# Strassen's products on 512-row blocks, and whole sequences convolved and routed at once, in a convolution with a gated mixture of experts

## The chip, the cores and the metric

The kernel runs on one core of a Trainium2 chip. The core has a matrix engine (PE, with its weight loads shown apart as PEld), a vector engine (DVE), a scalar engine (ACT), a general engine (POOL), a queue engine (SP), 16 DMA engines, an on-chip memory SBUF of 128 partitions, and PSUM, eight banks of 512 fp32 columns in which matmuls accumulate. The metric is the device time of one execution in microseconds; the kernel before takes 1325.93 us (median of three runs, 1324.46 to 1328.33).

## The reference

Eight sequences of 3,584 tokens with 192 channels are filtered and then go through one expert each:

```
out1[b,s,:]  = sum over k of softmax(weight)[head,k] * x[b, s-6+k, head]      # causal, 7 taps, 8 heads of 24 channels
logits       = out1 @ w_gate                  (8 experts)
fresh        = argmax(logits);  free = sigmoid(out1 @ w_local) < 0.5 or s == 0
expert[b,s]  = fresh if free else expert[b,s-1]                               # a chain along the sequence
out[b,s,:]   = softmax(logits)[expert] * (relu(out1 @ w1[expert]) @ w2[expert])   # 192 -> 1024 -> 192
```

All of it is fp32. There are 28,672 tokens.

## The kernel before

The tokens are cut into 16 groups of 1,792 (`NPART`, `PT`), two to a sequence. Groups 0 and 1 take a special path through PE (`wide`, `wide_route`), so that expert work can begin early. The other 14 take these stages:

- **Convolution** (`conv`, L366): each partition holds 14 successive tokens (`NT`) and their halo. For each of the 8 heads ACT writes the first tap (L377), and DVE adds six more, one instruction each (L387).
- **Logits** (`logits`, L565): DVE transposes the rows into `z` (L570), PE multiplies by the gate weights in 48 small matmuls (L580) into two tiles of the pool `hps_p`, ACT copies them out (L585), DVE turns them back (L588, L596).
- **Routing** (`route`, L601, and `table`): some 90 small DVE instructions find each token's expert and its slot in a table in DRAM, `slots`, in which each expert has its own stretch.
- **Puts** (`put`, L768): POOL scatters rows to `slots`, 128 at a time, by indirect DMA.

Expert work goes by blocks of rows of one expert. A unit is 128 rows; a block is one unit ("single") or two ("pair"). The list `blocks` is fixed when the program is built: 35 singles, then 87 pairs, then 20 singles, 229 units in all. Which expert a block belongs to is read from a table at run time. Two spare singles run at the end only if an entry asks for them. For each block SP loads the expert's weights (`load_w`, 1.5 MB, three blocks ahead, four buffers) and the rows (`load_rows`). PE transposes the rows (`turn`, L359), ACT copies them to `xT` (L949). `hidden` (L952) does the first layer: PE works with two tiles of 64 rows side by side, so 24 matmuls of 64 x 128 weights against 64 x 256 columns for a pair run as 12 concurrent couples; an fp32 matmul shows as two records. ACT applies relu (L968). `output` (L973) does the second layer: 16 matmuls of 192 columns per unit. ACT scales one half of the sum (L988), DVE scales and adds the other (L992), POOL scatters the result (L996).

The order is written out by hand in the main loop (L1138): every engine executes its instructions in the order in which the program issues them. Conv and route are generators; each `yield` gives a price in microseconds, and `step(t)` (L1037) issues about `t` us worth of them on DVE between the pieces of a block: 1.2 + 2.1 + 1.3 per single, 1.2 + 4.2 + 3.0 per pair. `ensure` (L1090) issues such work early and whole where a block needs a group that is not routed yet.

Of the kernel before, what the change touches and what calls it, by code (L numbers as in the profile page):

```python
# [33 lines left out]
NX = NT + HALO  # L34
# [4 lines left out]
KT = BT // P  # L39
# [4 lines left out]
EARLY = 3  # L44
SPARE = 2

# [5 lines left out]


ONE = [_sure(min(g + 1, EARLY) * PT, UT) for g in range(NPART)]
TWO = [_sure((g + 1) * PT - ONE[-1] * UT, BT) if g >= EARLY else 0 for g in range(NPART)]


HALF = 0.5
FULL = {0: ONE[0], HALF: _sure(PT + PT // 2, UT), **{g: ONE[g] for g in range(1, NPART)}}
REST = NU - ONE[-1] - 2 * TWO[-1]  # L60
# [21 lines left out]
def kernel(  # L82
# [13 lines left out]
    xs = ctx.enter_context(tc.tile_pool(name="xs", bufs=2))  # L96
    ys = ctx.enter_context(tc.tile_pool(name="ys", bufs=4))
# [3 lines left out]
    xp = ctx.enter_context(tc.tile_pool(name="xp", bufs=6))  # L101
    tp = ctx.enter_context(tc.tile_pool(name="tp", bufs=1))
    hp = ctx.enter_context(tc.tile_pool(name="hp", bufs=1))
    op = ctx.enter_context(tc.tile_pool(name="op", bufs=2))
    xps_p = ctx.enter_context(tc.tile_pool(name="xps_p", bufs=1, space=PSUM))
    hps_p = ctx.enter_context(tc.tile_pool(name="hps_p", bufs=4, space=PSUM))
    yps_p = ctx.enter_context(tc.tile_pool(name="yps_p", bufs=2, space=PSUM))
# [6 lines left out]
    def load_x(g):  # L114
        x_sb = xs.tile([P, NX, D], F32, name="x_sb")
        src = x[g // PER]
        win = bass.AP(tensor=src.tensor, offset=src.offset + g % PER * PT * D,
                      ap=[[NT * D, P], [1, NX * D]])
        nc.sync.dma_start(out=x_sb.rearrange("p t d -> p (t d)"), in_=win)
        return x_sb  # L120

    def load_b(g):

        x_sb = xs.tile([P, NX, D], F32, name="x_sb")
        xv = x_sb.rearrange("p t d -> p (t d)")[:, :NB * D].rearrange("p (b d) -> p b d", d=D)
        for b in (slice(0, NH), slice(NH, NB)):
            nc.sync.dma_start(out=xv[:, b, :], in_=xb[g, :, b, :])
        return xv
# [9 lines left out]
    with tc.tile_pool(name="scr", bufs=1) as scr:  # L138
# [4 lines left out]
        x_in = {0: load_b(0)}  # L143
        wg = cst.tile([P, 3 + DQ, Q], F32, name="wg")
        nc.sync.dma_start(out=wg, in_=wgl)
        x_in[1] = load_b(1)
# [43 lines left out]
    def z_tile():  # L190
        return yt.tile([P, 3 * NH * TB + NB * DR], F32, name="z")
# [3 lines left out]
    def wide(g, xv, y_sb, both):  # L195
# [58 lines left out]
        yr = zy[:TB, 3 * NH * TB:].rearrange("p (b d) -> p b d", d=DR)  # L254
# [17 lines left out]
        lt = sm.tile([P, NB, E + 1], F32, name="lt")[:TB]  # L272
# [9 lines left out]
    pi = cst.tile([P, 2], I32, name="pi")  # L282
# [83 lines left out]
    def conv(g, x_sb):  # L366
# [14 lines left out]
        for h in range(H):  # L381
            if h + 1 < H:
                first(h + 1)
# [850 lines left out]
```

## Time and profile before

| | |
|---|---|
| median of three runs | 1325.93 us |
| the profiled execution, its span | 1326.81 us, 1325.1 us |
| busy: PE, DVE, ACT, POOL | 1304.4, 778.3, 625.2, 480.4 us |
| granted PE clock | 0.998 |
| first expert matmul begins; last output matmul ends | 46.16; 1318.3 us |
| HBM read, written | 277.3 MB, 45.8 MB |

A group's line gives its source line, engine, operation, tiles, shapes and count, then busy time (the union of its instructions' intervals) and the mean duration of one. Matmuls overlap, so their mean is longer than busy time divided by count. The list by slices has one digit for each fortieth of the span, the busy share in tenths. The table by stages gives busy time and count per engine in a stretch. The timeline gives start, duration, engine, line and count of merged instructions.

### The profile page before, as it was taken

Reading aid. Unit: us, or ns where it says so; the run is one execution under the profiler, and the core shown is the slowest. Engines: PE = TensorE matmul, PEld = TensorE weight load, DVE = VectorE, ACT = ScalarE, POOL = GpSimd, SP = SyncE. Lnnn points to the kernel's source line nnn. Section 1 sums busy time; section 2 is a strip of 40 time slices with the busy share of each in tenths; the row PEclk is TensorE's granted clock in tenths of the full one; section 3 lists DMA queues with packets and bytes.
Section 4 is the critical chain, followed back from the end, with each engine's and each line's share of the span. In section 5 each row is a group of like instructions: output and inputs, shape, how many; then the busy total and the mean of one; then the engine's idle time right before and its main releaser. Section 6 shows DMA issues by size and latency. Waiting matters only on the chain. (4 is left out here: it accounts for less than half of the span.)

```text
span 1325.1 us, 41356 instructions
## 1 busy us (share of the span) xinstructions
PE 1304.4 (98%) x16682; PEld 1260.9 (95%) x16682; DVE 778.3 (59%) x2434; ACT 625.2 (47%) x1571; POOL 480.4 (36%) x520
## 2 busy tenths in 40 slices
PE   9899999999999999999999999999999999999997
PEld 7799999999999999999999999999999999999997
DVE  6888898977878787878777878785610000000000
ACT  5345555544454545444545454544444444444553
POOL 4445352534343434343434343434344212211111
PEclk9999999999999999999999999999999999999999
DMA  5789999967575757575757575756565555556893
GB/s 188 283 349 391 376 365 345 394 213 266 182 275 177 290 188 277 201 260 192 271 186 273 193 271 199 267 195 210 197 211 205 189 185 188 192 187 229 313 317 131
DMA packets 67298, 325.29 MB, mean 245 GB/s; under 512 B 12576, under 2 KB 38103, under 8 KB 47650
## 3 DMA queue, kind: packets, MB, share of 16 engines
q1 hardware_dynamic: 44784, 277.41, 58.4%
q0 software_dynamic: 22320, 45.22, 9.2%
q8 instruction: 133, 2.18, 0.7%
q14 instruction: 59, 0.48, 0.1%
q10 hardware_dynamic: 2, 0.00, 0.0%
HBM read 277.29 MB, written 45.77 MB: 244 GB/s over the span
## 5 line engine op out<-in xcount | busy, mean ns | idle before, releaser
L980 PE MATMUL yps<-wb,hT 64*128 64x192 f32 x7328 | 641.0, 325 | 5.8 <-ACT hT L968 2.8
L963 PE MATMUL hps<-xT,wb 64*128 64x256 f32 (+1 forms) x6816 | 637.2, 336 | 1.7 <-issue 1.4
L963 PEld LDWEIGHTS hps<-xT,wb 64*128 64x128 f32 x6816 | 589.1, 187 | 27.2 <-issue 4.0
L980 PEld LDWEIGHTS yps<-wb,hT 64*128 64x128 f32 x7328 | 602.8, 187 | 11.1 <-issue 4.6
L996 POOL DMA_INDIRECT out_dram<-o_sb,xg x229 | 232.3, 1014 | 605.7 <-DVE o_sb L992 533.9
L968 ACT ACTIVATE hT<-hps 128x512 f32<-128x512 f32 (+1 forms) x568 | 261.9, 512 | 361.4 <-PE hps L963 246.5
L387 DVE SCALAR_TENSOR_TENSOR y_sb<-x_sb,c,y_sb 128x336 f32<-128x336 f32 x672 | 376.5, 570 | 18.9 <-issue 0.8
L992 DVE SCALAR_TENSOR_TENSOR o_sb<-yps,xg,o_sb 128x192 f32<-128x192 f32 x229 | 87.5, 414 | 467.8 <-ACT o_sb L988 461.4
L775 POOL DMA_INDIRECT slots<-y_sb,posi x228 | 231.2, 1014 | 209.3 <-ACT xT L949 114.8
L988 ACT ACTIVATE o_sb<-yps,xg 128x192 f32<-128x192 f32 x229 | 86.9, 418 | 289.8 <-PE yps L980 287.4
L949 ACT COPY xT<-xps 64x256 f32<-64x256 f32 (+4 forms) x568 | 210.8, 371 | 11.7 <-issue 1.7
L377 ACT ACTIVATE y_sb<-x_sb,c 128x336 f32<-128x336 f32 x112 | 63.7, 581 | 0.0
L359 PEld LDWEIGHTS xps<-ident,xg 64*128 64x128 f32 (+1 forms) x916 | 57.0, 124 | 5.2
L359 PE MATMUL xps<-ident,xg 64*128 64x64 f32 (+1 forms) x916 | 60.0, 217 | 0.0
L570 DVE STREAM_TRANSPOSE z<-y_sb 128x768 f32<-128x768 f32 (+1 forms) x56 | 45.4, 853 | 0.4
L596 DVE COPY lt<-lq 32x36 f32<-32x36 f32 x224 | 40.8, 182 | 3.5
L580 PE MATMUL hps<-z,wg 64*32 64x128 f32 x1344 | 24.2, 272 | 1.2 <-issue 1.2
L580 PEld LDWEIGHTS hps<-z,wg 64*32 64x32 f32 x1344 | 19.2, 105 | 4.1 <-issue 2.9
L556 PE MATMUL yps<-y_sb,hot 112*128 112x194 f32 x64 | 12.6, 353 | 1.4 <-DVE hot L550 1.1
L556 PEld LDWEIGHTS yps<-y_sb,hot 112*128 112x128 f32 x64 | 11.3, 202 | 2.1 <-DVE hot L550 1.6
L672 DVE COPY bk<-so_far 1x32 f32<-1x32 f32 x56 | 12.3, 220 | 0.7
L588 DVE STREAM_TRANSPOSE lq<-ls 128x256 f32<-128x256 f32 x14 | 6.2, 441 | 10.9 <-ACT ls L585 10.9
(236 smaller groups left out, 358.0 us busy)
## 6 DMA issues: line engine op xcount, KB each, us to landing
wb<-in_w_dram SPq DMA_DIRECT2D x138, 1536.0 KB
x_sb<-in_x_dram SPq DMA_DIRECT2D x14, 1920.0 KB
xg<-slots SPq DMA_DIRECT2D x87, 195.0 KB
wb<-in_w_dram SPq DMA_DIRECT2D x12, 512.0 KB
xg<-slots SPq DMA_DIRECT2D x53, 97.5 KB
out_dram<-o_sb,xg POOLq DMA_INDIRECT x229
slots<-y_sb,posi POOLq DMA_INDIRECT x228
x_sb<-in_xb_dram SPq DMA_DIRECT2D x4, 768.0 KB
```

Of the source, the lines that this page charges most:

```text
L359: nc.tensor.transpose(to, src[rows], identity=ident[rows, rows])
L377: nc.scalar.activation(cols(h), chans(h, 0), Act.Copy, scale=c[:, h, 0:1])
L387: nc.vector.scalar_tensor_tensor(cols(h), chans(h, k), c[:, h, k:k + 1], cols(h), Alu.mult, Alu.add)
L570: nc.vector.transpose(z[:, t:u, :], y_sb[:, t:u, Y0:Y0 + D])
L775: ins = nc.gpsimd.indirect_dma_start(out=slots[:, :], in_=rows, in_offset=None, out_offset=bass.IndirectOffsetOnAxis(ap=to, axis=0)).ins
L949: copied = nc.scalar.copy(a, b)
L963: nc.tensor.matmul(hps[half][:, j, w], lhsT=wb[rows, f0:f0 + P], rhs=xT[rows, d, w], start=(d == 0 and j == 0), stop=(d == KD - 1), skip_g ...
L968: relu = nc.scalar.activation(hT[:, m:m + 2, w], hps[half][:, :, w], Act.Relu)
L980: nc.tensor.matmul(yps[half][:, k * D:(k + 1) * D], lhsT=hT[rows, m, k * P:(k + 1) * P], rhs=wb[rows, WA + m * D:WA + (m + 1) * D], start= ...
L988: nc.scalar.activation(o_sb[:, k, :], y[k][0], Act.Copy, scale=xg[:, k, 0:1])
L992: nc.vector.scalar_tensor_tensor(o_sb[:, k, :], y[k][1], xg[:, k, 0:1], o_sb[:, k, :], Alu.mult, Alu.add)
L996: sent = nc.gpsimd.indirect_dma_start(out=out, in_=o_sb[:, k, :], in_offset=None, out_offset=bass.IndirectOffsetOnAxis(ap=xg.bitcast(I32)[ ...
```

## The change

It has four parts, and the seven products are new code.

- **Blocks.** `EARLY` goes from 3 to 4: singles come first from four groups. The list is now 51 singles, 20 pairs, 31 blocks of four units ("fours"), 14 singles: again 229 units. The fixed list now assumes more than the worst case guarantees (`_likely` with `LEFT`...), and 28 spare singles stand under two conditions at the end.
- **Seven products.** For a four, `seven` replaces `hidden`: the first two chunks of 64 channels, the two halves of the hidden units and the two halves of the rows form a 2 x 2 by 2 x 2 product, done with 7 products in place of 8; the third chunk takes 4. `combine_x` makes the sums of inputs on DVE, `combine_w` those of weights on POOL, and DVE adds three of the results.
- **Sequences.** From group 4 on, a whole sequence (28 tokens per partition) is convolved and routed at once; inputs are loaded by quarters of the channels (`load_x`, issued by ACT within `taps`), and the first taps are issued in `taps`.
- **PSUM.** In place of `hps_p` (4 banks), `yps_p` and `xps_p` (2 each) there are four pools of one tile of two banks: `wps_p` (transposes), `xps_p` and `yps_p` (hidden), `zps_p` (output). The logits take the pool that `step` is given.

```diff
+NS = 2 * NT
-EARLY = 3
+EARLY = 4
+XG = 5
+FIRST = 8
+PAIRED = 20
+LEFT1 = 640
+LEFT2 = 1408
+LEFT = 2900
+LEFT3 = 1152
...
-    def load_x(g):
+    def load_x(u, queue=None):
...
+        (queue or nc.scalar).dma_start(out=x_sb.rearrange("p t d -> p (t d)"), in_=win)
...
+    def taps(most):
+        u = len(x_in)
+        if u < len(UNITS):
+            depth = 3 if UNITS[u][0] < EARLY else 2
+            if u - depth <= st["unit"] - (st["cgen"] is not None):
+                load_x(u)
+        for u in (st["unit"], st["unit"] + 1):
...
+                    tap(u, j)
...
+                nc.vector.scalar_tensor_tensor(cols, x_in[u][:, k:k + n, j * GS:(j + 1) * GS],
+                                               c[:, h, k:k + 1], cols, Alu.mult, Alu.add)
+                yield 0.6 if n == NT else 1.0
...
+            yield "pe"
+            both = st["bank"].tile([P, 2, 512], F32, name="ps")
+            lps = [both[:, half, :TQ * Q] for half in range(2)]
+            for b in range(DQ):
+                if b == DQ // 2:
+                    yield "half"
...
+    def combine_w(wb):
+        wt = hp.tile([P, 3, 2 * P], F32, name="wt")
+        b11, b12, b21, b22 = [wb[:, k * 2 * P:(k + 1) * 2 * P] for k in range(4)]
+        nc.gpsimd.tensor_tensor(wt[:, 1, :], b22, b12, op=Alu.subtract)
+        nc.gpsimd.tensor_tensor(b12, b12, b11, op=Alu.subtract)
+        nc.gpsimd.tensor_tensor(wt[:, 0, :], b22, b12, op=Alu.subtract)
+        nc.gpsimd.tensor_tensor(wt[:, 2, :], b21, wt[:, 0, :], op=Alu.subtract)
+        return wt
+
+    def combine_x(xT):
+        xc = hp.tile([P, 4, HU * P], F32, name="xc")
+        one, two = slice(0, HU * P), slice(HU * P, KT * P)
+        nc.vector.tensor_tensor(xc[:, 0, :], xT[:, 0, one], xT[:, 0, two], op=Alu.subtract)
+        nc.vector.tensor_tensor(xT[:, 0, two], xT[:, 0, two], xT[:, 1, two], op=Alu.add)
...
+    def seven(wb, wt, xT, xc, turn_next, weights_next):
...
+        def times(to, a, b, first=False):
+            for j in range(2):
+                for half, rows in halves():
+                    nc.tensor.matmul(to[:, half, j, :], lhsT=b[rows, j * P:(j + 1) * P],
+                                     rhs=a[rows, :], start=(first and j == 0), stop=True,
+                                     skip_group_check=True)
+        times(xb, a11, b11, True)
+        puts_by(nc.scalar.copy(h11, xb))
+        times(yb, s1, t1, True)
+        times(yb, a23, b32)
+        puts_by(nc.scalar.copy(h22, yb))
+        times(xb, s2, t2)
+        nc.scalar.copy(h12, xb)
+        times(wbk, a12, b21, True)
+        times(wbk, a13, b31)
+        step(SIDE[0])
+        nc.vector.tensor_tensor(h11, wbk, h11, op=Alu.add)
+        nc.scalar.activation(h11, h11, Act.Relu)
+        times(xb, s3, t3)
+        nc.vector.tensor_tensor(h22, xb, h22, op=Alu.add)
+        nc.scalar.activation(h22, h22, Act.Relu)
+        times(yb, s4, b22)
+        times(yb, s5, b32)
+        at = turn_next()
+        times(xb, a22, t4)
+        wt = weights_next()
+        times(xb, a23, b31)
+        nc.vector.tensor_tensor(h12, yb, h12, op=Alu.add)
+        puts_by(nc.scalar.activation(h12, h12, Act.Relu))
+        nc.scalar.activation(h21, xb, Act.Relu)
...
+    def output(n, wb, xg, hT, rows_next=None):
+        for part, h in enumerate(hT):
+            m = min(n, HU)
+            y_p = zps_p if part == len(hT) - 1 else yps_p
...
+            if rows_next and part == 0:
+                taps(min(n, 2))
+            step((1.3 if n > 1 or st["block"] else 0) if n < KT else SIDE[2 + part],
+                 wps_p if n < KT or part == 0 else None)
...
+            if part == 0 and rows_next:
+                rows_next()
+    SIDE = (2.0, 4.4, 1.6, 1.4)
...
+        if n == KT:
+            hT, at, wt = seven(wbs[i], wt, xT, xc, turn_next, weights_next)
+        else:
+            hT = hidden(n, wbs[i], xT, (1, 1) if i else (0, 0))
+            wt = weights_next()
+            at = turn_next()
...
+        step(2.4 if i == 0 else {1: 2.3, 2: 4.7, 4: SIDE[1]}[n], zps_p if n == KT else xps_p)
+        output(n, wbs.pop(i), xgs.pop(i), hT, rows_next)
...
+        if n < KT:
+            step(1.4 if n == 1 else 3.6)
```

## The prediction

> **What bounds the kernel now.** I read the busy shares and the forty slices first, then the groups by shape, then the stages, then PE's timeline.
>
> ```profile
> PE 1304.4 (98%) x16682; PEld 1260.9 (95%) x16682; DVE 778.3 (59%) x2434; ACT 625.2 (47%) x1571; POOL 480.4 (36%) x520
> ...
> PE   9899999999999999999999999999999999999997
> ...
> DVE  6888898977878787878777878785610000000000
> ```
>
> PE is busy in every slice; DVE is nearly full only up to a quarter of the span. Whether busy PE is also PE at its rate, the groups by shape and the timeline tell:
>
> ```profile
> L980 PE MATMUL yps<-wb,hT 64*128 64x192 f32 x7328 | 641.0, 325 | 5.8 <-ACT hT L968 2.8 <-DVE o_sb L992 1.9 <-issue 0.9
> L963 PE MATMUL hps<-xT,wb 64*128 64x256 f32 x4176 | 472.5, 376 | 0.0
> L387 DVE SCALAR_TENSOR_TENSOR y_sb<-x_sb,c,y_sb 128x336 f32<-128x336 f32 x672 | 376.5, 570 | 18.9 <-issue 0.8
> L968 ACT ACTIVATE hT<-hps 128x512 f32<-128x512 f32 x348 | 189.5, 595 | 288.9 <-PE hps L963 204.2 <-PE xps L359 78.9 <-issue 5.8
> L992 DVE SCALAR_TENSOR_TENSOR o_sb<-yps,xg,o_sb 128x192 f32<-128x192 f32 x229 | 87.5, 414 | 467.8 <-ACT o_sb L988 461.4 <-DMA xg<-slots 5.0 <-PE hps L963 0.9
> L968 ACT ACTIVATE hT<-hps 128x256 f32<-128x256 f32 x220 | 72.5, 381 | 72.5 <-PE hps L963 42.3 <-PE xps L359 14.4 <-ACT o_sb L988 7.8
> ```
>
> PE's own waits are 5.8 us of 641 in the second layer and nothing in the pairs' first layer; ACT and DVE wait for PE. Here is PE's timeline, first through two pairs, then two singles near the end:
>
> ```profile
> 271.04 5.34 PE L963 MATMUL hps<-xT,wb 64*128 64x256 f32 x47
> 276.04 0.39 PE L359 MATMUL xps<-ident,xg 64*128 64x64 f32 x5
> ...
> 281.70 5.34 PE L963 MATMUL hps<-xT,wb 64*128 64x256 f32 x47
> ```
> ```profile
> 1302.00 2.84 PE L963 MATMUL hps<-xT,wb 64*128 64x128 f32 x48
> ...
> 1307.44 2.84 PE L963 MATMUL hps<-xT,wb 64*128 64x128 f32 x48
> ```
>
> A pair takes 281.70 - 271.04 = 10.66 us, a single 5.44 us, always. A pair's first layer spans about 5.18 us for 12 couples (0.43 us per couple of 256 columns). The stages, with their busy times for PE, PEld, DVE, ACT and POOL, then clock, DMA share and GB/s, show where something else presses:
>
> ```profile
> 46.00:257.00 211.00, 203.97 (x3227) 198.43 (x3227) 185.67 (x562) 112.50 (x351) 95.22 (x94) 1.00 0.94 357
> 257.00:1209.00 952.00, 950.66 (x11505) 917.77 (x11503) 552.07 (x1742) 435.01 (x984) 343.70 (x339) 1.00 0.62 220
> 1209.00:1326.00 117.00, 109.07 (x1678) 108.48 (x1674) 9.10 (x22) 55.37 (x178) 21.44 (x22) 0.99 0.74 259
> ```
>
> The pairs' stage is PE alone: 87 x 10.66 = 927, 11 logits at about 1.9 (a pair with logits takes 12.5 us) = 21, leaving 4 of 952 us. The early singles are tighter: 35 x 5.44 = 190 and 3 logits at 2.3 = 7, so 14 of 211 us are lost there, with DVE 88% and DMA 94% busy. The last 20 singles lose nothing. So time is the count of matmuls, plus what the early singles lose.
>
> **What the Trainium skill says.** "FP8 and Floating Point Precision", section "TensorE Precision Notes", counts four passes for true fp32; the trace fits passes by columns, 0.43 us for 256 and about 0.33 for 192 (5.3 us for the pair's 16 couples), so a saved couple of 256 is worth its whole 0.43. "SBUF — State Buffer", section "SBUF: two separate sides", says that a POOL operation that reads SBUF and a DVE operation with two SBUF inputs lock each other out for the whole instruction. The trace before has too little POOL arithmetic to show this. "GPSIMD Engine Reference", section 3.1, prices an fp32 tensor_tensor at 4497 ns for 2,048 columns; the trace has only a POOL copy of 512 in 655 ns. "VectorE: DVE Perf Modes", on the SBUF errata, gives (N + 151)/0.96 ns for an fp32 tensor_tensor; the trace's scalar_tensor_tensor of 336 took 570 ns where that gives 507.
>
> **The change part by part.**
>
> *Units.* Both lists hold 229 units. Whether the tables fill is a matter of the seeded data: routed as the reference does, the experts get 3,274 to 4,253 tokens, every planned single, pair and four is full when its group is routed, and 1,152 tokens remain, exactly 14 singles. The 28 spares should not run.
>
> *Seven products, the gain.* A four's first layer is 11 products of two couples, 22 in place of 24: 2 x 0.43 = 0.85 us saved. Its second layer (64 matmuls) and 16 transposes are those of two pairs. So a four is 2 x 10.66 - 0.85 = 20.47 us. The new list against the old: 10 more singles, 67 fewer pairs, 31 fours: 10 x 5.44 - 67 x 10.66 + 31 x 20.47 = 54.4 - 714.2 + 634.6 = **-25.2 us**.
>
> *What a four asks of the others.* ACT: a 1,024-column read from PSUM, estimated from the two relu rows, (595 - 381)/256 = 0.84 ns per column, is about 1.02 us, or 0.97 with the uncontended 0.54 for 512 in the timeline. Three copies and four relus make 7, the four xT copies 2.7, o_sb 1.7, taps up to 1.9: 13 of 20.5 us. DVE: slope (570 - 414)/144 = 1.08 ns per column, so an add from PSUM of 1,024 is 1.3 us; three are 3.9; combine_x by the page's formula 5 x 0.42 = 2.1; four o_sb 1.7; the steps 2.0 + 4.4 + 1.6 + 1.4 = 9.4. Sum 17.1, and if POOL locks it out during combine_w, 4 x 0.56 (page, in proportion) to 4 x 0.8 more: 19.3 to 20.3. That just fits. POOL: up to 8 puts and 4 scatters at 1.01 plus 2.6 = 15.
>
> *Does any of it stand in PE's way?* Starting a four at 0 with products of 0.86: xb ends at 0.86, its ACT copy at 2.1, and PE writes xb again at 2.6: 0.5 spare. The copy of yb ends at 3.8, that of xb at 4.7; PE wants xb at 5.2: 0.4 spare. wbk ends at 5.2, the DVE adds of h11 and h22 at 6.7 and 8.0; transposes need wps at 7.8 and product a22 t4 needs xb at 8.4: 0.4 spare. h12 leaves yb at 9.3, wanted at 10.2. combine_x ends about 18.5 (20.5 with the lock), wanted at 21.3; combine_w has 10 us. So nothing stalls in the mean, with half a microsecond of slack at three places. In the fours that still carry conv and route (about 14, from the count below) I charge 0.25 us each, 3.5; bounds 0 and 1.5 each.
>
> *Conv and routing.* A 672-column tap is 570 + 336 x 1.04 = 920 ns for two of 570. The yields of a sequence sum to about 72 (48 conv, 24 route and tables) where two groups took 98. Counting steps against that, puts and blocks in order of issue, all groups are ready in time (one `ensure` at the first pair finds only a put missing), and conv and route are through by four number 14. DVE thus falls empty at about 830 us. Off PE's path this is worth nothing. Logits mostly get the bank wps after an output, whose next user is a whole first layer away: free. Two parts fall on xps, which the next block's first layer wants while ACT still does o_sb, a tap and the two copies: about 1 us each, 2.
>
> *Early singles.* Now 51 with DVE work, each carrying 2.3 + 1.3 + 1.4 = 5.0 in steps for 4.6. With o_sb that is 5.4 of 5.44 us, and only the logits' pauses let DVE breathe; DMA must bring 1.54 MB of weights, 0.1 rows and some 0.23 (was 0.18) of x per single. The first blocks already lose most of the 14 us, so 16 more singles at 0.2 each add 3; bounds 0 and 20 (0.4 each for 51). The moved x loads are issued by ACT behind o_sb; one that waited for DVE's last tap would hold ACT's relus and so PE, but that tap was issued before the output it follows. About 0 each; in the 20 bound.
>
> *Start and end.* Order and counts of the `wide` path stay; PSUM pools are only renamed, 0 +- 2. The last 14 singles are as before.
>
> *Sum.* Against the profiled execution: span 1325.1 - 25.2 + 3.5 + 2 + 3 = 1308.4. Its time lies 1.7 above its span and 0.9 above the median of the runs, so **1309 us**.
>
> **Rivals.**
>
> *The full gain.* Slack everywhere holds: 1325.1 - 25.2, in runs' terms 1301, perhaps less if the finer tiles of the hidden layer end the early 14 us. For it: the pairs lose nothing today. Against: three slacks of 0.4 us in each of 31 blocks.
>
> *DVE the bound in fours that carry conv.* The lock, or taps above 920 ns, make DVE need 21.4: 14 x 0.9 = 13 us more, 1321. For it: 19.3 to 20.3 of 20.5 above. Against: ACT and PE show no such pressure before, and DVE gets 17 fours without conv afterwards.
>
> *Slower: the chain of 1,024-column evacuations.* Today four half-banks rotate in the first layer; in `seven`, xb is written, read and written again with one buffer, three times. If copies plus their semaphores take 1.3 us longer than I put them, at any of those three places, PE loses 1.3 - 0.4 = 0.9 or more at each of two places, some 1.8 per four, 55 us, less where they overlap: about 1340. It decides from (25.2 - 5)/31 = 0.65 us of PE wait per four; then the gain is gone. For it: an ACT relu of 512 shows 0.54 or 0.60 depending on what else runs. Against: no L963 row waits for ACT now.
>
> *The singles press.* DVE or DMA falls behind over 51 singles at 0.4 each: 20 in place of 3, 1326, no change.
>
> **How the numbers follow.** A measurement here tells 0.3%, 4 us. Chances: 1309 (likeliest, its own range 1302 to 1319) 0.60; full gain 0.14; DVE-bound fours 0.10; evacuation chain 0.11; singles 0.05. The DVE-bound case at 1321 straddles the bound of 1322, half each side; of the singles' case 0.02 is no change and 0.03 slower. Faster: 0.60 + 0.14 + 0.05 = 0.79; within: 0.05 + 0.02 = 0.07; slower: 0.11 + 0.03 = 0.14. The range 1298 to 1330 leaves out the chain and the tails.
>
> **What will show it.** PE's first layer of a four should be 44 matmuls (88 records); fours should repeat every 20.5 us where DVE is empty; if PE rows of `seven` list idle time released by ACT copies or DVE adds, the chain rival is right, at 0.65 us per four and above the gain is lost. DVE should have no conv after about 830 us. In the first 350 us PE's idle time should not pass 20 us; weight loads landing late or o_sb of DVE releasing PE would show the press. More than 229 scatters of output would mean that spares ran, and each costs 5 us or more. I am wrong altogether if a couple of 256 columns costs more in `seven` than 0.43.

## The result, and the profile after

The changed kernel takes **1379.46 us** (median of four runs, 1377.82 to 1382.9), the kernel before beside it 1326.52: a ratio of **1.040** (95% interval 1.0376 to 1.043). It is slower by 4%, where 1.3% faster was forecast. The profiled execution has a span of 1376.1 us and a granted PE clock of 0.984. The runs below were made in six sessions, A to F, each with the kernel before beside it. Before took 1315 us in A and 1329 to 1332 in the others, so each ratio is against before in its own session. (The expectations call a session a job.)

The page of the changed kernel, parts 1 and 2:

```profile
PE 1307.0 (95%) x16674; PEld 1256.1 (91%) x16674; DVE 824.0 (60%) x1891; ACT 688.0 (50%) x1402; POOL 622.2 (45%) x650
...
PE   9899889998899999998999999998999999999997
```

PE issues eight records fewer than before and yet is busy 2.6 us longer, where the forecast took 25 us off; it is also idle for 69 us where it was idle for 21. So there are two losses: gaps, and matmuls that take longer. Two rows by shape of the changed kernel show where PE waits:

```profile
L1178 PE MATMUL ps<-wb,h 64*128 64x192 f32 x7328 | 641.4, 328 | 27.6 <-ACT h L1090 12.6 <-DVE o_sb L1193 8.3 <-issue 5.2
...
L426 ACT ACTIVATE y_sb<-x_sb,c 128x672 f32<-128x672 f32 x48 | 39.9, 864 | 22.9 <-DMA x_sb<-in_x_dram 22.9
```

In the second layer PE waited for 5.8 us before; now it waits for 27.6, 12.6 of them for ACT's relus. And ACT itself waits 22.9 us ahead of 48 first taps, for loads of x. Before, its taps waited for nothing:

```profile
L377 ACT ACTIVATE y_sb<-x_sb,c 128x336 f32<-128x336 f32 x112 | 63.7, 581 | 0.0
```

Next to that, the products do what was said of them. The timeline of PE late in the fours, where neither conv nor scatters of routed rows remain:

```profile
1106.50 2.78 PE L1136 MATMUL ps<-xT,wb 64*128 64x256 f32 x24
1109.09 1.06 PE L1136 MATMUL ps<-xc,wt 64*128 64x256 f32 x8
...
1126.91 2.78 PE L1136 MATMUL ps<-xT,wb 64*128 64x256 f32 x24
```

A four repeats after 20.41 us, with no wait of PE. Two pairs take 21.32. The gain per four is there, and it's lost elsewhere. The table sets the stages beside the sum of the prediction. A stage begins with the first matmul of its kind; a single is charged at 5.445 and a pair at 10.665 us, as the trace before has them, and logits at the prediction's 2.3 and 1.9:

| stage | the prediction's terms | predicted, us | measured, us |
|---|---|---|---|
| 51 early singles | 277.7 + 6 logits 13.8 + old loss 14 + 3 | 308.5 | 334.8 |
| 20 pairs | 213.3 + 4 logits 7.6 | 220.9 | 228.7 |
| 31 fours | 634.6 + 3.5 + 2 + 4 logits 7.6 | 647.7 | 680.3 |
| 14 last singles | 76.2 | 76.2 | 76.4 |

The differences of the first three, 26.3 + 7.8 + 32.6, are 66.7 of the 67.7 us by which the span missed 1308.4.

**What stops the singles.** The chain that ended last, of the changed kernel, between 195 and 213 us (start, length, what):

```profile
195.84 9.84 DMA x_sb<-in_x_dram
...
205.70 0.02 ACT y_sb L426
...
206.47 0.37 ACT h L1090
...
206.88 5.49 PE ps L1178 x32
```

An x load of 9.84 us lands; only then does ACT run the tap that needs it, and the relus of the current block, which have nothing to do with x, stand behind that tap in ACT's order. PE waits 3.88 us for them. Then 32 matmuls take 5.49 us instead of 2.82; PE's timeline of the block ahead and of this one:

```profile
197.40 2.82 PE L1178 MATMUL ps<-wb,h 64*128 64x192 f32 x32
...
206.88 5.49 PE L1178 MATMUL ps<-wb,h 64*128 64x192 f32 x32 [3.88 <-ACT h L1090]
```

The table by windows of the same kernel gives the reason in its PEclk column (the third number from the end):

```profile
192.00:202.90 10.90, 10.90 (x168) 10.84 (x168) 8.54 (x12) 4.92 (x17) 7.04 (x6) 1.00 0.96 354
202.90:206.90 4.00, 0.12 (x6) 0.02 (x2) 2.51 (x4) 1.20 (x3) 0.38 (x1) 0.87 0.87 336
206.90:212.20 5.30, 5.30 (x34) 5.30 (x36) 0.62 (x1) 1.79 (x7) 1.92 (x2) 0.50 0.98 339
```

After the gap the granted clock is 0.50 for a while. "TensorE: Matmul & The Clock Gate" of the Trainium skill, section "HAM oscillation — how this bites in real kernels", says just that: PE left idle for a window of about 3.4 us is throttled to half. The trace agrees in the main: the gap of 3.88 us is followed by 6.83 us at half, and half-clock stretches in the stages come in 3.41 us or twice that. (Shorter waits bring it too; see the end.) The prediction didn't use this page, so it priced each gap at its own length.

**What stops the fours.** The timeline of PE in one of the fours that scatter and don't convolve any more, and POOL beside it:

```profile
890.93 0.53 PE L400 MATMUL ps<-ident,xg 64*128 64x64 f32 x12
891.88 0.25 PE L400 MATMUL ps<-ident,xg 64*64 64x64 f32 x2 [0.42 <-issue]
893.30 0.26 PE L400 MATMUL ps<-ident,xg 64*64 64x64 f32 x2 [1.17 <-issue]
894.77 1.53 PE L1136 MATMUL ps<-xT,wt 64*128 64x256 f32 x8 [1.21 <-DVE h L1153]
```

```profile
886.11 0.97 POOL L1198 DMA_INDIRECT out_dram<-o_sb,xg  x1 [0.30 <-DVE inn L922]
887.38 0.96 POOL L872 DMA_INDIRECT slots<-y_sb,posi  x1 [0.30 <-ACT h L1144]
888.65 0.96 POOL L872 DMA_INDIRECT slots<-y_sb,posi  x1 [0.30 <-issue]
889.92 0.96 POOL L872 DMA_INDIRECT slots<-y_sb,posi  x1 [0.30 <-issue]
891.18 0.96 POOL L872 DMA_INDIRECT slots<-y_sb,posi  x1 [0.30 <-issue]
```

Six scatters follow one another at 1.27 us (the first, at 884.83, isn't shown). PE's idle time at 891.5 and 892.1 is put down to issue: it waits for nothing that the profile shows. ACT's timeline has 2.46 us of the same before 890.40. This four takes 26.4 us. In all, PE's waits for issue in the stage of the fours come to 13.1 us.

### The profile page after: what moved, and what is told of

Its sections match the earlier page's. It is cut to its first block, busy times and chain, and to the rows that moved or that the text cites. A ratio compares the mean times of both kernels' runs of the same rounds, so it can differ in the third digit from the quotient of the medians.

```text
span 1376.1 us, 40772 instructions
## 1 busy us (share of the span) xinstructions
PE 1307.0 (95%) x16674; PEld 1256.1 (91%) x16674; DVE 824.0 (60%) x1891; ACT 688.0 (50%) x1402; POOL 622.2 (45%) x650
## 4 chain that ended last, share of the span: by engine, by line
PE 85%; DVE 5%; DMA 5%; issue 3%; POOL 1%; ACT 1%; another core or an unknown queue 0%; DVEq 0%; POOLq 0%; ACTq 0%; SPq 0%
PE ps L1178 42%; PE ps L1136 21%; PE ps L1086 17%; DMA x_sb<-in_x_dram 3%; PE ps L665 2%; PE ps L400 2%; DVE y_sb L464 1%; DMA slots<-y_sb,posi 1%; DVE h L1153 1%; PE hps L249 1%; POOL slots L872 1%; DMA out_dram<-o_sb,xg 0%; PE hps L194 0%; ACT h L1090 0%
## 5 line engine op out<-in xcount | busy, mean ns | idle before, releaser
L1178 PE MATMUL ps<-wb,h 64*128 64x192 f32 x7328 | 641.4, 328 | 27.6 <-ACT h L1090 12.6
L1178 PEld LDWEIGHTS ps<-wb,h 64*128 64x128 f32 x7328 | 609.5, 189 | 37.7 <-ACT h L1090 19.9
L464 DVE SCALAR_TENSOR_TENSOR y_sb<-x_sb,c,y_sb 128x672 f32<-128x672 f32 (+1 forms) x384 | 322.7, 848 | 35.2 <-ACT y_sb L426 21.4
L1086 PE MATMUL ps<-xT,wb 64*128 64x128 f32 (+1 forms) x4080 | 299.3, 298 | 3.5 <-issue 2.1
L1193 DVE SCALAR_TENSOR_TENSOR o_sb<-ps,xg,o_sb 128x192 f32<-128x192 f32 x229 | 87.7, 413 | 353.2 <-ACT o_sb L1186 346.8
L1086 PEld LDWEIGHTS ps<-xT,wb 64*128 64x128 f32 x4080 | 281.5, 188 | 16.1 <-issue 7.2
L1186 ACT ACTIVATE o_sb<-ps,xg 128x192 f32<-128x192 f32 x229 | 87.3, 418 | 332.0 <-PE ps L1178 286.9
L1090 ACT ACTIVATE h<-ps 128x256 f32<-128x256 f32 (+1 forms) x340 | 127.5, 431 | 152.3 <-PE ps L1086 109.5
L1064 ACT COPY xT<-ps 128x128 f32<-128x128 f32 (+2 forms) x464 | 194.3, 419 | 10.5 <-issue 3.2
L1136 PE MATMUL ps<-xT,wb 64*128 64x256 f32 x1488 | 182.8, 379 | 1.1 <-issue 1.0
L1136 PEld LDWEIGHTS ps<-xT,wb 64*128 64x128 f32 x1488 | 157.9, 189 | 7.6 <-issue 2.9
L1136 PE MATMUL ps<-xc,wt 64*128 64x256 f32 x496 | 67.7, 381 | 1.6 <-issue 1.6
L426 ACT ACTIVATE y_sb<-x_sb,c 128x672 f32<-128x672 f32 (+1 forms) x64 | 48.9, 793 | 24.2 <-DMA x_sb<-in_x_dram 24.1
```

The source lines that it names most:

```text
L426: nc.scalar.activation(got[g][:, :, Y0 + h * GS:Y0 + (h + 1) * GS], x_in[u][:, :n, j * GS:(j + 1) * GS], Act.Copy, scale=c[:, h, 0:1])
L464: nc.vector.scalar_tensor_tensor(cols, x_in[u][:, k:k + n, j * GS:(j + 1) * GS], c[:, h, k:k + 1], cols, Alu.mult, Alu.add)
L1064: copied = nc.scalar.copy(a, b)
L1086: nc.tensor.matmul(hps[:, half, j, :], lhsT=wb[rows, f0:f0 + P], rhs=xT[rows, d, :], start=(d == 0 and j == 0), stop=(d == KD - 1), skip_g ...
L1090: relu = nc.scalar.activation(hT[two][:, half], hps[:, half], Act.Relu)
L1136: nc.tensor.matmul(to[:, half, j, :], lhsT=b[rows, j * P:(j + 1) * P], rhs=a[rows, :], start=(first and j == 0), stop=True, skip_group_che ...
```

## The experiments

Three theories came from that reading. **A**: taps that wait for x loads to land hold ACT's relus, and so PE. **C**: scatters in a row stall the issue of the other engines. **Rivals**: 51 singles overload DVE or DMA (B, F, G below), or DVE and the evacuations bound the fours (D). Lengths of stages in the text are from the traces, as in the table above, one trace for each run; sums of waits are counted in the same traces, over gaps of more than 0.15 us.

### Taps held back

```diff
-        if ... or st["block"] <= x_at[u]:
+        if ... or st["block"] <= x_at[u] + (1 if x_at[u] >= 0 and blocks[st["block"]][1] == 1 else 0):
```

> The change, with the taps that wait for a newly loaded part of x held back one block more while the blocks are singles (about one block, 5.4 us, more for the transfer; nothing is left out of the computation). Theory A (the early singles lose their time because ScalarE waits, in its own order, in a tap for an x load of up to 10 us, with the relus of the next block behind it): ScalarE's idle time released by the x loads falls from 23 us to 5 or less, TensorE's gaps of 2 to 5 us between 46 and 381 us go, and with them the half clock that follows; about 20 us less, 1358. Rival B (51 singles fill VectorE and the DMA engines, and the wait for x only shows where the backlog lands): the stage keeps its length and the time stays within 4 us of 1379.

Measured in session A: 1331.32 us, 1.0124 of before (1.0108 to 1.0141). The row of the first taps by shape, in this kernel:

```profile
L426 ACT ACTIVATE y_sb<-x_sb,c 128x672 f32<-128x672 f32 x48 | 39.3, 862 | 4.2 <-DMA x_sb<-in_x_dram 4.1
```

ACT's wait fell from 22.9 to 4.2 us, as A said. The stage of the singles took 311.1 us, where the two other variants of the session, which leave the singles as the change has them, took 334.8 and 338.5: 24 to 27 us less. The gain in the total can't be read off 1379, since before itself was 11 us faster in A. B is wrong as the cause of this loss: the stage didn't keep its length. What is left of it, some 20 us, is looked at below.

### Scatters spread in the fours

```diff
-        puts_by(nc.scalar.copy(h11, xb))
+        nc.scalar.copy(h11, xb)
...
-        puts_by(nc.scalar.copy(h22, yb))
+        put(nc.scalar.copy(h22, yb))
...
-        nc.scalar.activation(h11, h11, Act.Relu)
+        put(nc.scalar.activation(h11, h11, Act.Relu))
...
-        puts_by(nc.scalar.activation(h12, h12, Act.Relu))
+        put(nc.scalar.activation(h12, h12, Act.Relu))
...
+                if n == KT:
+                    put(sent_by)
...
-            if n == KT or (len(to_put) > NT // 2 and n == 2):
+            if n == KT:
+                put(copied)
...
```

> The change, with the scatters of routed rows of a four sent one at a time at five places of the block instead of in twos behind four places (nothing is left out). Theory C (four to six scatters in a row on GpSimd's queue hold up the issue of instructions on TensorE, ScalarE and VectorE at once, and the half clock that follows doubles the loss): idle time of TensorE put down to issue falls from about 18 us to 5 or less and the fours between 610 and 1030 us lose 15 to 20 us less; about 1362. Rival D (those fours lose their time to VectorE, to its lock with GpSimd or to the chain of evacuations): the issue gaps may move, the time stays within 4 us of 1379.

Measured in session A: 1340.98 us, 1.0206 (1.0187 to 1.0224); the fours took 651.3 us. That looks like C. But the kernel with taps held back sent its scatters in bundles in the same session, and its fours took 657.6, with next to no stalls: the stalls were absent from every trace of session A, bundled or not (PE's waits for issue sum to 0.5 to 5.8 us there, to 18.4 in the change). Its timelines of POOL and PE, at the same scatters, which come one four later here:

```profile
879.39 0.96 POOL L872 DMA_INDIRECT slots<-y_sb,posi  x1 [0.30 <-ACT h L1144]
880.66 0.98 POOL L872 DMA_INDIRECT slots<-y_sb,posi  x1 [0.30 <-issue]
881.94 0.96 POOL L872 DMA_INDIRECT slots<-y_sb,posi  x1 [0.30 <-issue]
883.20 0.96 POOL L872 DMA_INDIRECT slots<-y_sb,posi  x1 [0.30 <-issue]
```

```profile
875.16 2.75 PE L1136 MATMUL ps<-xT,wb 64*128 64x256 f32 x24
...
882.93 0.63 PE L400 MATMUL ps<-ident,xg 64*128 64x64 f32 x16
883.40 1.09 PE L1136 MATMUL ps<-xT,wt 64*128 64x256 f32 x8
```

The same row of two outputs and four puts at the same pace, and PE runs through it; this four takes 20.42 us (875.16 to 895.58). So the run told nothing on C, only that bundles need not cost anything. PE itself kept its pace from session to session: the last 14 singles took 76.3 us in A and 76.4 or 76.5 in the others.

### The change without fours

`FIRST = 16` and `PAIRED = 999` in place of 8 and 20: 51 singles, 81 pairs, 16 singles.

> The change without its fours: whole sequences, loads, logits and banks as changed, but the list is 51 singles, 81 pairs and 16 singles (nothing is left out). Two pairs cost 0.85 us more than a four, so 31 fours given up cost 26 us. If the fours are innocent of the loss and it sits in the singles and in what the new order of conv and loads does, the time is 1379 + 26 = 1405. If the 36 us or so that the stage of the fours loses against 31 x 20.42 (logits aside) come from the fours themselves (bursts of scatters, the late first four), these go too: 1365 to 1375. The early singles lose their 40 to 57 us in either case.

Measured in session A: 1360.33 us, 1.0329 (1.0282 to 1.0377). By its total neither branch can be decided, as their base of 1379 was measured in another session. By stages it can: 81 pairs took 878.1 us (81 x 10.66 + 7 logits = 876.8, so nothing is lost) and the last 16 singles 87.1, 965.2 together. With fours and spread scatters the same work took 220.5 + 651.3 + 76.3 = 948.1. The fours keep 17 of their 26 us where nothing stalls; the rest goes at the first four, which takes 30.1 us there.

### The kernel before with bundles

```diff
-        hT = hidden(n, wbs[i], xT, (1, 1) if i else (0, 0))
+        hT = hidden(n, wbs[i], xT, ((1, 1) if n == 1 else (0, 0)) if i else (0, 0))
-            if len(to_put) > NT // 2 and n == KT:
-                put(copied)
+            if n == KT and i % 2 == 0:
+                for _ in range(5): put(copied)
```

> The kernel before, with the scatters of routed rows in the pairs not spread but sent five in a row at the end of every other pair (nothing is left out). Theory C: each burst holds up the issue of TensorE, ScalarE and VectorE for 1 to 3 us, and a half clock follows each; some 20 bursts make 40 to 90 us more, 1365 to 1415. Rival: a burst on GpSimd's queue by itself costs the other engines nothing, since nothing waits for it; within 4 us of 1326.

Measured in session A: 1319.38 us, 1.0039 (1.0025 to 1.0053). By itself this would have been the end of C. The same kernel once more, in session C:

> The kernel before with its scatters bundled in fives, once more. The first time (1.004 of before) no trace of that job showed idle time put down to issue beyond 5 us, neither here nor in the changed kernel's variants; in the second job all of them showed 13 us and more. If this job is like the second, theory C expects stalls of 0.4 to 1 us behind the bundles here too, and 1.012 or more; if bundles cost nothing even there, 1.004 again and theory C is wrong. If the job is like the first, it tells nothing new.

Measured: 1432.25 us, **1.0755** (1.0719 to 1.0791). The row of the pairs' first layer, first in session A, then in session C:

```profile
L963 PE MATMUL hps<-xT,wb 64*128 64x256 f32 x4176 | 467.7, 376 | 0.0
```

```profile
L963 PE MATMUL hps<-xT,wb 64*128 64x256 f32 x4176 | 511.6, 382 | 41.3 <-issue 39.9
```

One program, one row: 40 us of waiting for nothing and 44 us more of busy time. The pairs took 951.1 us in A and 1046.8 in C; 44 us of them at half clock in C, which costs about 22 of the 96. Both sessions are recorded on chip number 0. Of the 32 rows of six or seven scatters in A none brought a wait for issue; all 17 such rows in C did, 1.1 to 2.7 us each up to 3 us behind the row. A bundle of session C, in the timelines of POOL and PE:

```profile
531.17 0.96 POOL L775 DMA_INDIRECT slots<-y_sb,posi  x1 [4.56 <-ACT xT L949]
...
536.22 0.96 POOL L775 DMA_INDIRECT slots<-y_sb,posi  x1 [0.30 <-issue]
537.49 0.99 POOL L996 DMA_INDIRECT out_dram<-o_sb,xg  x1 [0.30 <-DVE y_sb L387]
```

```profile
538.38 0.59 PE L963 MATMUL hps<-xT,wb 64*128 64x256 f32 x2 [0.70 <-issue]
539.81 0.59 PE L963 MATMUL hps<-xT,wb 64*128 64x256 f32 x2 [0.84 <-issue]
541.22 1.16 PE L963 MATMUL hps<-xT,wb 64*128 64x256 f32 x8 [0.82 <-issue]
```

PE first stalls six scatters into the row. In session F the same number of scatters went three at a time, at every pair (`for _ in range(3)`):

> The kernel before with its scatters of routed rows three in a row at the end of every pair (five in a row with the two of the output) in place of five at every other pair. If the price is one per bundled scatter, it is that of the fives again, 1.07 to 1.08 of before in a job with issue stalls. If the first few of a row are free and only those behind them stall the other engines, as the stalls in the fives begin with the fifth or sixth (2.5 us per bundle of seven), it is 1.00 to 1.03. In a job without stalls 1.00 to 1.01.

Measured: 1338.92 us, 1.0056 (1.0041 to 1.0071), the pairs 956.5 us. Waits for issue were there, but few: 3.7 us in the row of the pairs' first layer. The fives were not run in F, so that F is a session with stalls is inferred: ACT waited for issue nine times there (7.2 us), and never in the four traces of session A. If it is one, the price is not one per scatter: the first four or five of a row are nearly free, and what comes behind them is not. Counted from the traces (a scatter belongs to a row if it starts within 0.6 us of the end of the one ahead, from 46 us on): the kernel before has no row longer than 4, the threes none longer than 5. The fives have 32 rows of 6 or 7 in the session without stalls. The changed kernel has 18 rows of 6 to 24. That is what the bundles of two at each place did, together with the outputs. Length alone doesn't tell the price. In the changed kernel the six rows of 7 to 24 ahead of the fours, 95 scatters that came 1.54 to 1.68 us apart in the mean of a row, brought PE 2.0 us of waits for issue; the twelve rows of six in the fours, 72 scatters 1.27 to 1.53 us apart, brought 14.1. Whether the pace or the kind of block makes the difference wasn't tested.

### The change again, and the two edits together

> The changed kernel itself once more, beside the same runs of the kernel before as the three below. In the first runs the held-back taps gave 1.012 of before, the spread scatters 1.021 and the list without fours 1.033, where the change itself had shown 1.040; but before was 11 us faster there than in the first comparison. If the change stays at 1.035 to 1.045 of before, the differences are the edits'. If it comes out at 1.02 to 1.03, half of them belong to the day. Its trace tells whether the idle time of TensorE that is put down to issue behind bursts of scatters comes back: 15 us or more if it is the kernel's own, under 6 if it was a matter of that one run.

Measured in session B: 1382.21 us, 1.0395 (1.0355 to 1.0435); the stalls are back (PE waits 17.6 us for issue), and the fours take 682.4 us.

The taps held back and the scatters of a four spread, both as above:

> Both edits together: taps held back one block more and the scatters of a four one at a time. If each removes a loss of its own, the gain of both adds up: against the held-back taps alone (1.0124 of before) some 10 us less, 1.005. If spread scatters do nothing where nothing stalls on issue, 1.012 again.

Measured in session B: 1375.38 us, 1.0337 (1.0295 to 1.0379): not 1.005. Against the change in the same session the singles fell by 27 us, to 321.8, and the fours by 10, to 672.7, but the pairs rose from 229 to 249, with stalls behind their own bundles (9.7 us of waits for issue, 2.8 in the change) and with work that was put off.

### The first four

In `seven` the step is skipped when the block before isn't a four, and so is the step at the end of the last pair; logits no longer take the bank that the next first layer wants.

```diff
-        step(SIDE[0])
+        if blocks[st["block"] - 1][1] == KT:
+            step(SIDE[0])
...
-        step(..., zps_p if n == KT else xps_p)
+        step(..., zps_p if n == KT else None)
...
-        if n < KT:
+        if n < KT and n_next != KT:
```

> The change, with two small edits on work of VectorE that lies ahead of TensorE's: no conv or route at the end of the last pair before the first four nor in the middle of that four (12 conv operations of 0.95 us stood ahead of the adds there), and logits only in the PSUM bank that comes free after an output, no longer in the bank that the next block's first layer wants. Theory: the first four falls from 31 to 21 or 22 us and waits of TensorE for the copies of logits go, 8 to 10 us less than the change itself. Rival: the conv that is put off costs the same elsewhere: within 3 us of the change.

What suggested it is in the first four of the changed kernel; DVE's timeline, and PE's:

```profile
610.63 6.49 DVE L464 SCALAR_TENSOR_TENSOR y_sb<-x_sb,c,y_sb 128x672 f32<-128x672 f32 x6
...
618.65 2.70 DVE L652 STREAM_TRANSPOSE z<-y_sb 128x768 f32<-128x768 f32 x3
621.27 1.19 DVE L1150 TENSOR_TENSOR h<-ps,h 128x1024 f32<-128x1024 f32 x1
```

```profile
622.52 1.12 PE L400 MATMUL ps<-ident,xg 64*128 64x64 f32 x16 [4.68 <-DVE h L1150]
```

Measured in session B: 1387.46 us, 1.0453 (1.0411 to 1.0495). The first four fell from 34.4 to 24.2 us, but the next two rose from 23.4 and 21.2 to 26.6 and 23.8, and fours further on took the rest; the stage is 681.4 against 682.4. The rival is right: the conv that was put off cost the same elsewhere.

### All edits, three ways of placing scatters

> All four edits together: taps held back, scatters one at a time, the first four cleared of conv, logits only in the bank that comes free after an output. From the trace of the held-back taps alone (1331 where before took 1315) go 5.7 + 2 us at the first four, 8.9 us of waits for the copies of logits and 2 us of half clock: 1313, about before's own 1315. If the 25 us of Strassen's products are there at all, the sum must come to before or below; at 1325 or more there is a loss that I have not named.

Measured in session B: 1362.15 us, 1.026 (1.0223 to 1.0297). It misses 1313; the session had stalls (PE waits 17.6 us for issue), and 7.4 us went to rows of a four whose last scatters were late. The expectations below call this kernel c1.

```diff
-                step(4.2, wps_p, True)
+                if st["routed"] < g:
+                    step(4.2, wps_p, True)
...
+            if n == KT and part == 1:
+                puts_by(sent_by)
...
+                if n == 2 and k == m - 1:
+                    puts_by(sent_by)
```

> The kernel with all four edits, and two more: where the rows of a coming block wait only for scatters, these are sent without 17 us of conv and routing ahead of them (four forced steps of 4.2 at the last early single), and the scatters are placed so that a pair sends at most two in a row and the last group of the fours is through earlier (nothing is left out). Against c1 (1.026 of before): the wait of 7.4 us for rows in the fours goes, 6 us in the pairs, some 5 us at the last early single: about 1.012 where the issue stalls are, about 1.000 where they aren't. If it stays at 1.02 or more, none of these was on the path.

Measured in session C (c2): 1378.36 us, 1.0375 (1.0325 to 1.0425), worse than c1, though in another session. The wait of 7.4 us for rows went, but PE waited 34.0 us for issue: behind two outputs, two scatters make four in a row, and with those at the next place six.

Then one put at each place, and none in pairs behind an output:

```diff
-            for _ in range(shares[two] if n == 2 else (0, sum(shares))[two]):
-                put(relu)
-            if two and (n == 2 or st["block"] % 2):
-                more(relu, n)
+            if shares[two]:
+                put(relu)
...
-        nc.scalar.activation(h21, xb, Act.Relu)
+        put(nc.scalar.activation(h21, xb, Act.Relu))
```

> The change with its scatters apart everywhere: a single sends one behind each relu of its hidden layer, a pair one more behind the copies of the transposed rows, a four six, each behind another ScalarE or VectorE instruction; rows that wait only for scatters no longer force conv and routing; logits keep to the bank that comes free after an output and the first four is cleared of conv, as before. Nothing is done to the x loads. Theory C, in a job with stalls: the fours fall from 680 to 655 to 665 us, TensorE's idle time put down to issue below 8 us, the singles stay at 335 to 348; 1.020 to 1.028 of before. If the fours stay above 672 and the stalls remain, it is not the distance between scatters that counts. In a job without stalls: within 8 us of the change's own run, from the first four and the logits alone.

Measured in session D: 1381.91 us, 1.0374 (1.0334 to 1.0413), against 1.0438 of the change itself there:

> The changed kernel itself, as the base for the two below on the same chip. In a job with issue stalls 1.04 of before as twice already, its fours 680 us. In a job without them, theory C says that the fours take 655 to 660 us as they did with the taps held back (657.6), the singles still 335 to 340, and the whole 1.02 to 1.03 of before; if it is 1.04 even there, the stalls were not part of the loss.

The change took 1384.6 us, 1.0438 (1.0395 to 1.048). With scatters apart the fours fell from 683.2 to 670.7 us, 12.5 where C had promised 18 to 28, and the pairs rose from 227.2 to 239.3, because the scatters were late. PE's waits in the trace with scatters apart:

```profile
PE ps L1177 <- ACT h L1090: 22.3, 16, 5.8
PE ps L400 <- DMA xg<-slots: 10.5, 2, 5.3
PE ps L1134 <- issue: 9.0, 13, 1.1
```

The first line is A's wait, which this edit doesn't touch (in the change it is 11.9 us here, beside 10.3 for DVE's o_sb). The second is grown from 2.7 us. The third is a part of the waits for issue, which come to 13.3 us against 20.5 in the change; C had said under 8. Under half of them, 6.8 us, fall within the nine rows of six and more that are left or in the 4 us behind them; with all four edits it was 5.4 of 17.6. So long rows don't account for all of these waits, and what brings the others is open.

> The same with the taps that wait for x held back one block more as well. Theory A and C together: the singles fall by 24 to 29 us against the run with scatters apart alone; 1.000 to 1.008 of before in a job with stalls. If it stays at 1.02 or more as c1 and c2 did, there is a third loss in the singles that neither names.

Measured in session D (c3): 1363.18 us, 1.0271 (1.0235 to 1.0306), 19 us less than with scatters apart alone, and the singles fell from 339.8 to 320.0. A holds in a third session, with 20 us in place of 24 to 29; 1.000 to 1.008 was too good.

Last, the same with the scatters on time again (c4):

```diff
+                if n == 2 and k == 0:
+                    puts_by(early_o)
...
+                if n == KT and st["routed"] == LATER[-1]:
+                    more(copied)
```

> c3 with its scatters as fast as the change sends them: in pairs two more behind ScalarE's first o_sb, in the fours of the last group one more behind the copies. By count no rows are put off in the pairs any more. Expected against c3 (1.027): the 10 us of TensorE waiting for rows go, and 8 us of half clock in the pairs with them: 1.012 to 1.018 of before in a job with issue stalls. If it stays at 1.025, scatters that are on time and scatters that are apart can't be had together in this order of the work. In a job without stalls 0.990 to 1.000.

Measured in session E: 1371.92 us, 1.0331 (1.031 to 1.0351). The late rows are gone, and PE's waits for issue grew in their place, from 16.7 us in c3 to 28.3:

```profile
PE ps L1134 <- issue: 9.6, 14, 1.1
PE ps L1177 <- issue: 8.8, 16, 1.2
```

> The changed kernel itself, as the base for c4. In a job with issue stalls 1.040 to 1.044 as three times before; in one without them 1.02 to 1.03, its fours at 655 to 660 us and its singles still at 335 to 340.

The change itself there: 1383.0 us, 1.04 (1.0377 to 1.0423), its singles 344.5 us where c4 took 318.3. So scatters that are on time and scatters that are apart were not had together in this order of the work: the 28 scatters of a sequence become due at once, where half-sequences gave 14. No version that was run beats the kernel before. Whether c1 would in a session like A was not measured; an estimate is some 1317 us, from the pairs and fours with spread scatters and the singles with held-back taps there, where before took 1315.

### What else sits in the singles

With the taps held back, the singles still take 311 to 328 us where their matmuls and logits are 291.5. Two runs in session C, one execution each, leave work out on top of c2:

```diff
+        part = (n + HALO) * DH // (1 if queue or blocks[st["block"]][1] > 1 else 4)
```

> c2 with three quarters of each x load left out while the blocks are singles (the convolution then works on what lay there before, so routing and the end of the kernel differ; only the stage of the 51 early singles is read). With the taps held back this stage takes 311 to 323 us where 51 x 5.445 + 13 for logits are 291. Theory F: the rest is DMA at its limit (94 to 96% busy, 1.54 MB of weights per single and x beside it): 0.17 MB less per single of 1.9, and the stage falls by 10 us or more. Rival G (VectorE sets the rest): within 3 us of c2's stage.

```diff
             for k in range(1, KC):
+                if k % 2 or blocks[st["block"]][1] > 1:
```

> c2 with half of VectorE's taps left out while the blocks are singles (so outputs and routing differ; only the stage of the 51 early singles is read). Rival G: VectorE, 85% busy there, sets what is lost beside the x waits: with 3 of 6 taps gone the stage falls by 10 us or more against c2. Theory F (DMA at its limit): within 3 us of c2's stage.

Measured: 319.7 and 320.1 us, against 328.4 of c2. Both are less, by more than 3 and by less than 10, so neither theory's own test is met; c1 and c3, with nothing left out, took 322.8 and 320.0. So neither the bytes of x nor DVE's taps are shown to set the rest. A part of it is waits for issue (13.9 us of PE's in this stage of c2, 7.5 and less in c1, c3 and c4); the rest is open.

## Why the prediction was wrong, step by step

- **Seven products, the gain** (20.47 us per four, 25.2 in all): right. Clean fours repeat at 20.41 us. 229 outputs were scattered, so no spare ran; conv was off DVE by 796 us (830 said).
- **What a four asks of the others; does it stand in PE's way**: right where tested. Adds of 1,024 took 1.22 us (1.3 said), `combine_x` 0.42 to 0.46 each, POOL's sums 758 to 828 ns, where "GPSIMD Engine Reference", section 3.1, gave 0.56 in proportion and 0.8 was the upper bound. The lock between POOL and DVE is seen: DVE's taps of 672 columns took 0.92 us on their own and 1.21 in the mean (up to 1.46) where one of POOL's sums ran beside them; the adds, with one input in PSUM, took 1.22 either way. No wait in a clean four; the chain of evacuations, the rival for slower, isn't there.
- **DVE the bound in fours that carry conv** (rival): plain in the first four, 10 us above the rest; clearing that one of conv moved the loss to later fours.
- **Conv and routing**: ready in time, as counted. It counted scatters by their sum ("up to 8 puts and 4 scatters ... = 15" of 20.5 us) and not by how they follow one another. This is **the first step that failed**: the stage was charged 0.25 us per four with conv and 2 for logits, 5.5 in all, and lost 38.1. In session A, where the fours are the change's own but don't stall, the stage took 657.6, so 23 to 26 us of it go with the stalls; setting scatters apart where there were stalls took 10 to 12.5 of them away. That close rows of scatters bring stalls is shown by the fives of session C; why some sessions have none is not known, nor what brings the waits outside of such rows. The kernel before, whose rows are no longer than four, had been read for what scatters take and not for what their distance spares.
- **Early singles**: right in asking whether the moved x loads hold ACT, wrong in the answer, and this is **the second step that failed**. "that tap was issued before the output it follows. About 0 each" looked at what a load waits for before it starts. The wait is at the other end: the first tap that *reads* the load comes one block later, 5.4 us, and the load took 9.84 in the case shown, with DMA 89% busy over the stage. 3 us became 29, and held-back taps gave 20 to 27 of them back in four sessions. The rival "the singles press" had the place and the sign, but the wrong cause: it charged the throughput of DVE and DMA.
- **Pairs**: 7.8 us that the sum hadn't. 6.4 of them are in one pair at 513.6 us, behind a row of 17 scatters and partly at half clock: it took 18.65 us, and 12.28 in the run of session A with the same singles and pairs.
- **The clock**: no step had it. In the changed kernel's singles, pairs and fours the clock was at half for 34 us, which costs about 17 (an estimate: half of that time). A gap of 3.9 us thus cost 6.6.

The first of the two steps argued from a sum: the work had room in the mean of a block, and stood in a line at the moment. The second looked at the order in which loads start and not at the order in which they are read.

## What to carry to other kernels

Ask of each in-order engine not only when its loads are issued but which instruction reads them first, and what stands behind that one; a tap that waits for DMA belongs behind the work on the critical path, or a block later. Count scatters by how many follow one another at POOL's own pace, not by their sum; rows of up to five cost little in the kernel before, and longer rows with pauses between the scatters brought little wait in the changed one. Measure in more than one session, since a layout can look free in one and cost 7.5% in the next. Where PE is the bound, price a gap of 3 us or more at its length and a half-clock window on top, and look for the half clock behind rows of shorter waits too.

## What the runs showed of the hardware

- Indirect scatters at POOL's own pace (1.27 us apart) can stall the issue of PE from about the fifth or sixth of a row on. The same program showed this in session C (1046.8 us for the pairs) and not in session A (951.1). There it is PE almost alone (47.2 us of waits for issue, ACT 1.8); in the changed kernel ACT and DVE waited for issue too (43.0 and 11.0 us, PE 18.4). What differs between sessions, and by what path POOL's scatters reach the others' issue, was not found. Late instruction fetch doesn't show as the reason: of PE's 42 waits for issue of 0.4 us and more in the fives of session C, 31 had no packet of instruction fetch in the 3 us ahead of them.
- Gaps and the clock, counted in all twenty traces from 45 us to the last output: behind gaps of PE of 3 us and more a half-clock stretch began in 43 of 44, at the latest 3.5 us after the gap, behind 2 to 3 us in 15 of 32, behind 1.5 to 2 us in 2 of 37. Short waits in a row bring it as well: in the fives of session C, 11 of 12 stretches began where PE had no gap of 1 us but had been idle for 1.15 to 2.4 of the last 3.4 us. So the window of some 3.4 us that the Trainium skill names in "TensorE: Matmul & The Clock Gate" is not a safe limit.
